# A list scheduler counts 32-wide matmuls at a quarter of their work, sends outputs ahead at low activity, and gets new settings per stretch

## The chip, the cores and the metric

The kernel runs on one core of one Trainium2 chip. The metric is the time of one execution on the device, in microseconds (us). The kernel before takes 723.09 us, the median of 3 runs (721.96 to 723.36).

## What is computed

The reference is an attention stage with 32 inducing vectors, done twice, and then a gated feed-forward layer on its output:

```python
B, N, m, C = (4, 12416, 32, 128)
def mab(q, kv):
    s = scale * (q @ kv.transpose(0, 2, 1))
    s = s - s.max(-1, keepdims=True)
    a = np.exp(s)
    a /= a.sum(-1, keepdims=True) + 1e-09
    return a @ kv
h = mab(I, x)             # I: 32 inducing vectors for each of 4 batches
attn = mab(x, h)          # 4 * 12416 rows of 128
gate = 1.0 / (1.0 + np.exp(-(attn @ w_gate)))    # w_gate, w_val: 128 x 1536
val = attn @ w_val
return (gate * val @ w_out).astype(np.float32)   # w_out: 1536 x 128
```

Since `attn` is `a2 @ h`, the kernel multiplies the 32-row `h` by the weights once for each batch (`hw`, made at L395) and multiplies the 32 attention weights `a2` of each row by that.

## The kernel before

**The tiles.** The 49664 rows are 96 blocks of 512 rows, and a 97th of what is left over (128 rows of each batch). A block has 12 chunks (`NJ`), each 128 of the 1536 hidden columns. A chunk goes through four engines:

- PE (TensorE) makes `v_ps` and `g_ps`, one matmul each with 32 rows of contraction, 128 columns of weights and 512 moving columns (a "fill", `emit_fill`, L1178);
- ACT (ScalarE) takes the tanh of `g_ps` into `t` (L1192);
- DVE (VectorE) makes `u = (t + 1) * v` (`emit_product`, L1204), straight from PSUM;
- PE adds the chunk into the block's output with four 128x128x128 matmuls (`acc_ps`, `emit_out`, L1229). When all 12 chunks are in, ACT copies the block out at half its value (L1246) and SP stores it (L1253).

Chunks are taken in steps of two and one by turns (`step`, L1339): a step of two has one product of 128x1024, a step of one a product of 128x512. Each size has one PSUM buffer for `v` and one for `g`, so a fill of a size waits until the product before it of that size has been read. If two chunks are left at the end, the last step departs from the turns.

**Side work.** Between the blocks of one batch the first stage of the next batch is done: scores of 16 tiles of rows (`s_ps`, L294, 32 columns of weights and 512 moving columns), maximum, exp, a transpose by DMA, and sums (`hp_ps`, L354, 128 rows of contraction, 32 columns of weights; with each of 128 moving columns goes one of a single column). Then the second-stage weights `a2` of the batch's groups of four blocks are made on PE, ACT and POOL (GpSimd), and SP transposes them by DMA into `a2r` (L571), which the fills read. Some chunks are put "aside" (`maybe_aside`, L1513): their product is made by ACT and POOL instead of DVE (`side_g_ps`, `side_v_ps` at L1555, `side_t` at L1565 to L1576). There are 23 of these.

**What sets the order.** All of this is issued by a list scheduler that runs when the kernel is built. It keeps a model clock for each engine and calls `do_pe`, `do_act`, `do_dve` and so on for the engine that is free first; the instructions are then emitted in order of their modelled start. Each engine's queue runs in that order on the chip. The rules are steered by numbers (`knob`), which `SETTINGS` changes at every eighth block (`STRETCH = 8`). In `do_pe` (L1760) the order of choice is: fills that are due, then side work (`side_`), then output matmuls (`run_out`), then a "pulse" (`emit_pulse`, L1742: a matmul of zeros into the open output bank). `queued() > knob["outq"]` makes outputs `pressed`: they then go ahead of side work, unless that has waited longer than `age`.

A pulse is sent when PE has nothing to do and `recent(tau)` (L1752) is below `guard`. `recent` sums the `work` of the PE operations that started in the last 3413 ns:

```python
for start, work in reversed(spent):
    if start < tau - 3413:
        break
    busy += work
```

The `work` of an output matmul is 0.95 of its cost of 56, which is 53; a fill is counted at 53 for each chunk; a group's scores at 852, half a group's sums at 430 (8 matmuls of 128 moving columns and 8 of one), half of `hw` at 850.

Of the kernel before, what the change touches and what calls it, by code (L numbers as in the profile page):

```python
# [21 lines left out]
SWAPS = True  # L22
STRETCH = 8
SETTINGS = (
    dict(most=6, margin=300, loose=150, lead=1000, calm=26, outq=40, quiet=1, slack=90,
        guard=1800, hold=22, eager=300, keep=0, pace=9999, soft=80, push=36, patience=6000,
        hurry=100, window=320, age=3500, ahead=21),
    dict(quiet=3, push=14),
    dict(eager=100, push=30),
    dict(lead=1900, quiet=1, eager=300, soft=20, push=36),  # L30
    dict(soft=80),
    dict(),
    dict(),
    dict(calm=22),
    dict(calm=26, hold=26),
    dict(hold=22, push=26),
    dict(push=36),
    dict(),
)
TIMES = (  # L40
# [36 lines left out]
def kernel(  # L77
# [508 lines left out]
    early, middle, last = arrival[:EARLY], arrival[EARLY:-1], arrival[-1]  # L586
# [246 lines left out]
    ROW, COL, FULL = "row", "col", "full"  # L833
    SWITCH = 100
    FILL = 216
# [13 lines left out]
    knob = dict(SETTINGS[0])  # L849
# [46 lines left out]
    def add(eng, cost, lag, emit, deps=(), after=None, kind=FULL, opens=False, closes=False, rank=None, work=None):  # L896
        op = Op(eng, cost, lag, emit, deps, after, kind, work=work)
        op.opens, op.closes = opens, closes
        op.rank = len(ranks) if rank is None else rank
        ranks.append(op)  # L900
        wait[eng].append(op)
        for d in op.deps:
            if d.done is None:
                d.users.append(op)
                op.left += 1
        if op.left == 0:
            live[eng].append(op)
        return op
# [27 lines left out]
    loaded, turned, hw_op, hT_op, a2_op, s1_used = {}, {}, {}, {}, {}, {}  # L936
# [3 lines left out]
    def op_stage1(b, s, score_at, sum_at, st):  # L940
        full = groups[s][1] == GC
        ng, w, R = s1_dims(s)

        def score():
            st["s1"] = s1_score_pe(b, s, "m")

        def weigh():
            st["a1T"] = s1_exp(b, s, st["s1"])

        a = add("PE", FILL, 380, score, [turned[b, s]], score_at, COL, opens=True, work=852)  # L950
        heads.append(a)
        n = 512 if full else 128
        m_ = add("DVE", 64 + 1.047 * n, 84 + 1.047 * n, lambda: s1_max(b, s, st["s1"]), [a])
        x = add("ACT", 600 if full else 250, 700 if full else 342, weigh, [m_], closes=True)
        if full:
            def turn():
                st["a1"] = s1_turn_dma(b, s, st["a1T"])
            c = add("SP", 80, 3400, turn, [x])
        else:
            def turn_pe():  # L960
                st["aT"] = s1_turn_pe(b, s, st["a1T"])
            def turn_copy():
                st["a1"] = s1_turn_copy(s, st["aT"])
            t_ = add("PE", 60, 240, turn_pe, [x], None, FULL, opens=True)
            heads.append(t_)
            c = add("DVE", 81, 160, turn_copy, [t_], closes=True)

        def part(k0, k1):
            if k0 == 0:
                st["hp"] = side_tile([P, C + 1], F32, "hp_ps")  # L970
            s1_sum_pe(b, s, st["a1"], st["hp"], k0, k1)

        p0 = add("PE", 160, 300, lambda: part(0, 2), [c, loaded[b, s]], sum_at, COL, opens=True, work=430)
        heads.append(p0)
        p1 = add("PE", 160, 300, lambda: part(2, 4), [p0], None, COL, work=430) if full else p0
        s1_used[b, s] = add(
            "ACT", 147, 260, lambda: s1_sum_keep(b, s, st["hp"]), [p1], closes=True
        )

    def op_combine(b, join_at, total_at, fill_at):  # L980
# [44 lines left out]
        def part(hf):  # L1025
            st["hw_ps"] = hw_fill(b, hf, side["m"])
# [8 lines left out]
        a = add("DVE", 71, 160, least, [s1_used[b, s] for s in range(NS)], join_at)  # L1035
# [10 lines left out]
        )  # L1046
        last = None
        for hf in range(2):
            f = add("PE", 170, 330, lambda hf=hf: part(hf), [hT_op[b], last], fill_at[hf], COL, opens=True, work=850)
            heads.append(f)  # L1050
            last = add("ACT", 360, 485, lambda hf=hf: keep(hf), [f], closes=True)
        hw_op[b] = last
# [699 lines left out]
    def recent(tau):  # L1752
        busy = 0
# [4 lines that stand above are left out]
        return busy  # L1758

    def do_pe(tau):  # L1760
# [7 lines left out]
        if rG is not None and (nxt["G"] < 2 or (st is None)):  # L1768
            s = max(tau + pe_switch(ROW), rG)
# [11 lines left out]
        if rG is not None and sg["n"] < nxt["V"] + 2 and rG <= tau + pe_switch(ROW):  # L1781
            s = max(tau + pe_switch(ROW), rG)
# [4 lines left out]
        for o in live["PE"]:  # L1787
            r = ready(o)
# [103 lines left out]
```

## Time and profile before

| | before |
|---|---|
| median of 3 runs | 723.09 us |
| the profiled execution, its own time | 717.5 us |
| its span, first to last instruction | 715.7 us |
| mean granted TensorE clock | 0.994 |
| DVE busy, share of the span | 98% |
| ACT busy | 95% |
| PE busy | 98% |
| POOL busy | 67% |
| SP's stores of a block, issue to landing | 2.2 us |

The profiled execution is 5.6 us shorter than the median of the runs. In a row of a group, the number after the bar is the group's busy time in us, then the mean of one instruction in ns, then the time that the engine stood idle before these instructions, with what ended it. In a table of stretches, each engine has its busy time in us in the stretch and in brackets the instructions that reach into it; PEclk is the granted clock of the stretch.

### The profile page before, as it was taken

Reading aid. Unit: us, or ns where it says so; the run is one execution under the profiler, and the core shown is the slowest. Engines: PE = TensorE matmul, PEld = TensorE weight load, DVE = VectorE, ACT = ScalarE, POOL = GpSimd, SP = SyncE. Lnnn points to the kernel's source line nnn. Section 1 sums busy time; section 2 is a strip of 40 time slices with the busy share of each in tenths; the row PEclk is TensorE's granted clock in tenths of the full one; section 3 lists DMA queues with packets and bytes.
Section 4 is the critical chain, followed back from the end, with each engine's and each line's share of the span. In section 5 each row is a group of like instructions: output and inputs, shape, how many; then the busy total and the mean of one; then the engine's idle time right before and its main releaser. Section 6 shows DMA issues by size and latency. Waiting matters only on the chain.

```text
span 715.7 us, 21551 instructions
## 1 busy us (share of the span) xinstructions
PE 700.7 (98%) x8449; PEld 408.2 (57%) x8449; DVE 698.1 (98%) x862; ACT 677.8 (95%) x1037; POOL 483.0 (67%) x747
## 2 busy tenths in 40 slices
PE   8999999999999999999999999999999999999997
PEld 4455565555555555555555655565555555555555
DVE  6899999999999999999999998999999999999997
ACT  4699999999999999999999998999999999999996
POOL 4587586688776774879895582777677588588211
PEclk9999999999999999999999998999999999999999
DMA  9797596225377625242357623121221120320211
GB/s 210 114 187 140 115 164 133 61 75 102 94 156 140 116 69 112 68 104 69 89 99 161 123 47 60 60 62 45 67 71 60 46 76 30 76 69 37 77 45 46
DMA packets 118181, 65.76 MB, mean 92 GB/s; under 512 B 101408, under 2 KB 102208, under 8 KB 118080
## 3 DMA queue, kind: packets, MB, share of 16 engines
q1 hardware_dynamic: 112176, 50.90, 30.5%
q0 software_dynamic: 5584, 13.34, 11.7%
q8 instruction: 66, 1.08, 0.6%
q14 instruction: 35, 0.29, 0.1%
q10 hardware_dynamic: 320, 0.15, 0.1%
HBM read 27.80 MB, written 25.43 MB: 74 GB/s over the span
## 4 chain that ended last, share of the span: by engine, by line
PE 83%; DVE 6%; ACT 5%; DMA 3%; issue 2%; POOL 1%; DVEq 0%; ACTq 0%; POOLq 0%
PE acc_ps L1229 41%; PE v_ps L1178 31%; PE g_ps L1178 6%; DVE u L1204 5%; ACT t L1192 5%; PE s_ps L429 2%; DMA xn<-in_x_dram 2%; PE hp_ps L354 1%; DMA a2r<-a2n 1%; PE s_ps L294 1%; PE side_g_ps L1555 0%; DVE nm L306 0%; PE xt_ps L615 0%; ACT o L1246 0%; POOL hpart L658 0%
## 5 line engine op out<-in xcount | busy, mean ns | idle before, releaser
L1204 DVE SCALAR_TENSOR_TENSOR u<-t,v_ps 128x1024 f16<-128x1024 f16 x761 | 666.3, 948 | 3.4 <-PE g_ps L1178 2.0
L1192 ACT ACTIVATE t<-g_ps 128x1024 f16<-128x1024 f32 x760 | 583.4, 832 | 16.9 <-ACT t L1192 5.8
L1229 PE MATMUL acc_ps<-wo,u 128*128 128x128 f16 x4564 | 389.3, 221 | 0.9 <-ACT o L1246 0.5
L1229 PEld LDWEIGHTS <-u 128*128 128x128 f16 x4564 | 262.6, 98 | 165.7 <-issue 162.8
L1178 PE MATMUL v_ps<-a2r,hwt 32*128 32x512 f16 (+1 forms) x1165 | 292.2, 377 | 5.2 <-DVE u L1204 2.0
L1178 PE MATMUL g_ps<-a2r,hwt 32*128 32x512 f16 (+1 forms) x1165 | 290.8, 375 | 0.0
L1178 PEld LDWEIGHTS <-hwt 32*128 32x128 f16 x2354 | 103.5, 91 | 98.7 <-issue 15.9
L560 POOL TENSOR_TENSOR a2n<-e,rs 128x2048 f16<-128x2048 f16 (+1 forms) x23 | 83.9, 3648 | 1.8
L533 POOL TENSOR_TENSOR near<-sme,minus 128x16 f32<-128x16 f32 (+1 forms) x22 | 65.2, 2964 | 1.8
L1246 ACT ACTIVATE o<-acc_ps 128x512 f32<-128x512 f32 x96 | 58.5, 610 | 0.0
L484 POOL TENSOR_SCALAR rise<-rise 128x256 f32<-128x256 f32 (+6 forms) x110 | 51.0, 463 | 9.4
L482 POOL TENSOR_TENSOR rise<-sc 128x256 f32<-128x256 f32 (+1 forms) x22 | 16.2, 737 | 58.2 <-ACT sc L472 58.1
L1576 POOL TENSOR_TENSOR side_t<-side_t,side_v 128x512 f16<-128x512 f32 x23 | 29.2, 1267 | 33.3 <-ACT side_v L1573 17.7
L1569 POOL TENSOR_SCALAR side_t<-side_t 128x512 f32<-128x512 f16 x23 | 34.4, 1497 | 19.4 <-ACT side_t L1565 19.2
L508 POOL TENSOR_TENSOR sum<-e 128x256 f32<-128x256 f16 (+1 forms) x23 | 15.4, 671 | 35.6 <-ACT e L500 33.4
L486 POOL TENSOR_TENSOR top<-top,rise 128x128 f32<-128x128 f32 (+3 forms) x88 | 28.3, 322 | 7.1
L508 POOL TENSOR_TENSOR sum<-sum 128x128 f32<-128x128 f32 (+3 forms) x92 | 28.3, 308 | 7.0
L482 POOL TENSOR_TENSOR rise<-top 128x128 f32<-128x128 f32 (+3 forms) x88 | 27.2, 309 | 6.7
L490 POOL TENSOR_TENSOR sc<-sc,top 128x512 f32<-128x512 f32 (+1 forms) x22 | 23.8, 1084 | 1.7
L319 ACT ACTIVATE a1T<-s_ps,nm 128x512 f16<-128x512 f32 (+1 forms) x26 | 16.9, 651 | 3.0 <-DVE nm L306 2.9
L429 PE MATMUL s_ps<-hT,xT 128*128 128x32 f16 x388 | 17.8, 177 | 0.1
L429 PEld LDWEIGHTS <-xT 128*128 128x128 f16 x388 | 14.0, 96 | 6.5 <-issue 6.1
(157 smaller groups left out, 340.9 us busy)
## 6 DMA issues: line engine op xcount, KB each, us to landing
out_dram<-o SPq DMA_DIRECT2D x96, 256.0 KB, 2.2
xn<-in_x_dram POOLq DMA_DIRECT2D x18, 512.0 KB, 6.9
xn<-in_x_dram POOLq DMA_DIRECT2D x3, 544.0 KB, 7.6
xn<-in_x_dram POOLq DMA_DIRECT2D x3, 256.0 KB, 12.6
xn<-in_x_dram SPq DMA_DIRECT2D x1, 576.0 KB, 4.9
xn<-in_x_dram SPq DMA_DIRECT2D x1, 512.0 KB, 4.0
a2r<-a2n SPq DMA_TRANSPOSE x27, 4.5
wg<-in_moe_w_gate_dram POOLq DMA_DIRECT2D x1, 384.0 KB, 11.6
```

What stands on the lines that cost most here:

```text
L429: nc.tensor.matmul(s2[:, j, :], xT[b][:, c + j, :], hT16[b][:], start=(j == 0), stop=whole and j == j1 - 1, skip_group_check=True,)
L482: nc.gpsimd.tensor_tensor(out=r, in0=far, in1=near, op=ALU.subtract)
L484: nc.gpsimd.tensor_scalar_max(out=r, in0=r, scalar1=0.0)
L508: nc.gpsimd.tensor_tensor(out=d[:, 0:n, :], in0=src[:, :, 0:w], in1=src[:, :, w : 2 * w], op=ALU.add)
L533: nc.gpsimd.tensor_tensor(out=near[:, 0:n], in0=sme[:, 0:n], in1=minus1[:, 0:n], op=ALU.pow)
L560: eng.tensor_tensor(out=a2n[:, 0:n, :, :], in0=e.unsqueeze(2).to_broadcast((P, n, 4, m)), in1=rs.unsqueeze(2).unsqueeze(3).to_broadcast((P ...
L1178: nc.tensor.matmul(pt[:, k, col : col + nb * P], hw[b][r : r + 32, j // 2, :], a2r[r : r + 32, o : o + nb, :].rearrange("p j t -> p (j t)" ...
L1192: st["tanh"] = nc.scalar.activation(out=st["t"][:], in_=st["g"][:], func=AF.Tanh, scale=0.5)
L1204: u = nc.vector.scalar_tensor_tensor(out=st["u"][:, :, c:e], in0=st["t"][:, :, c:e], scalar=1.0, in1=st["v"][:, :, c:e], op0=ALU.add, op1= ...
L1229: nc.tensor.matmul(accs[i][(q // 2) % len(accs[i])][:, q, :], u[:, ts(q, P)], wo16[:, item["j"], :], start=begins, stop=last, skip_group_c ...
L1246: nc.scalar.mul(out=o32[:], in_=accs.pop(i)[0][:], mul=0.5)
L1569: nc.gpsimd.tensor_scalar_add(out=st["t1"][:], in0=st["t"][:], scalar1=1.0)
```

## The change

The change does four things, all in the scheduler:

- a group's scores count 213 instead of 852, half a group's sums 107 instead of 430, half of `hw` 160 instead of 850: rows times columns of the array, as fills were counted already;
- outputs are also `pressed` when `recent(tau)` is below a new knob `warm` (1500, and 1700 in one stretch);
- the numbers in `SETTINGS` are chosen anew: among others `guard` is 1700 in the first stretch and then 1800, `lead` 1900 for nearly all of the way (which puts chunks aside only when ACT is that far ahead), and `age` 2500 in the first;
- with these, 24 chunks are put aside instead of 23, at other places, and the order of nearly every stretch differs.

```diff
 SETTINGS = (
-    dict(most=6, margin=300, loose=150, lead=1000, calm=26, outq=40, quiet=1, slack=90,
-        guard=1800, hold=22, eager=300, keep=0, pace=9999, soft=80, push=36, patience=6000,
-        hurry=100, window=320, age=3500, ahead=21),
...
+    dict(most=6, warm=1500, margin=300, loose=150, lead=1900, calm=26, outq=40, quiet=1,
+        slack=90, guard=1700, hold=22, eager=300, keep=0, pace=9999, soft=80, push=26,
+        patience=6000, hurry=100, window=320, age=2500, ahead=21),
...
-        a = add("PE", FILL, 380, score, [turned[b, s]], score_at, COL, opens=True, work=852)
+        a = add("PE", FILL, 380, score, [turned[b, s]], score_at, COL, opens=True, work=213)
...
-        p0 = add("PE", 160, 300, lambda: part(0, 2), [c, loaded[b, s]], sum_at, COL, opens=True, work=430)
+        p0 = add("PE", 160, 300, lambda: part(0, 2), [c, loaded[b, s]], sum_at, COL, opens=True, work=107)
...
-        p1 = add("PE", 160, 300, lambda: part(2, 4), [p0], None, COL, work=430) if full else p0
+        p1 = add("PE", 160, 300, lambda: part(2, 4), [p0], None, COL, work=107) if full else p0
...
-            f = add("PE", 170, 330, lambda hf=hf: part(hf), [hT_op[b], last], fill_at[hf], COL, opens=True, work=850)
+            f = add("PE", 170, 330, lambda hf=hf: part(hf), [hT_op[b], last], fill_at[hf], COL, opens=True, work=160)
...
-        pressed = r is not None and r <= tau + 30 and queued() > knob["outq"]
+        pressed = r is not None and r <= tau + 30 and (queued() > knob["outq"] or recent(tau) < knob["warm"])
```

In the whole program PE has 4656 output matmuls as before (96 of them from chunks aside, before 92), two fills less at L1178 and two more at L1555, and 13 pulses instead of 3. Seven of the pulses, of 512 columns each, stand between the fills near the end of block 83 (counted from 0), just ahead of the four output matmuls of a chunk aside. DVE has 380 products of 128x1024 and 379 of 128x512 as before, and the last step has one chunk instead of two.

**PE, in the first stage of the last batch (block 56 counted from 0; now 56 and 57), two groups' sums.** `hp_ps_9660` and `hp_ps_9714` are the sums of two groups, `u16_...` a product, `hwt` and `a2r` what the fills read. Before:

```order
L1229 MATMUL acc_ps_9590<-wo16_108,u16_9607 128x128
...
L354 MATMUL hp_ps_9660<-xn_3_5414,a1_9404 32x128
...
L1178 MATMUL v_ps_9679<-a2r_9118,hwt_7620 128x512
...
L354 MATMUL hp_ps_9660<-ones16_121,a1_9404 32x1
...
L1178 MATMUL v_ps_9702<-a2r_9118,hwt_7620 128x512
...
L354 MATMUL hp_ps_9714<-xn_3_5414,a1_9519 32x128
...
L1229 MATMUL acc_ps_9590<-wo16_108,u16_9621 128x128
L1178 LDWEIGHTS hwt_7620
L1178 MATMUL v_ps_9734<-a2r_9118,hwt_7620 128x512
```

The same two groups now (here `hp_ps_9718` and `hp_ps_9814`):

```order
L354 MATMUL hp_ps_9718<-ones16_121,a1_9310 32x1
L1229 LDWEIGHTS u16_9663
L1229 MATMUL acc_ps_9604<-wo16_108,u16_9663 128x128
L1178 LDWEIGHTS hwt_7480
L1178 MATMUL v_ps_9776<-a2r_9265,hwt_7480 128x512
...
L1229 MATMUL acc_ps_9604<-wo16_108,u16_9675 128x128
...
L1229 MATMUL acc_ps_9787<-wo16_108,u16_9702 128x128
...
L1229 MATMUL acc_ps_9787<-wo16_108,u16_9715 128x128
...
L354 MATMUL hp_ps_9814<-xn_3_5378,a1_9539 32x128
```

Before, the second group's sums follow the first's with one step's fills between them and no output matmul, and one output matmul stands in the middle of the second group. Now 16 output matmuls stand between the two groups, and one between the halves of each.

**DVE, the end of the program.** The rows are the last products and the last copy out. Before:

```order
L1204 SCALAR_TENSOR_TENSOR u16_15562<-t16_15524,v_ps_15555 128x512
L1204 SCALAR_TENSOR_TENSOR u16_15590<-t16_15550,v_ps_15564 128x1024
L1204 SCALAR_TENSOR_TENSOR u16_15623<-t16_15587,v_ps_15611 128x2x384
L1204 SCALAR_TENSOR_TENSOR u16_15623<-t16_15587,v_ps_15611 128x2x128
L1243 TENSOR_SCALAR o32_15651<-acc_ps_15584 128x256
```

Now:

```order
L1204 SCALAR_TENSOR_TENSOR u16_15611<-t16_15555,v_ps_15584 128x512
L1204 SCALAR_TENSOR_TENSOR u16_15625<-t16_15582,v_ps_15613 128x1024
L1204 SCALAR_TENSOR_TENSOR u16_15646<-t16_15608,v_ps_15629 128x384
L1204 SCALAR_TENSOR_TENSOR u16_15646<-t16_15608,v_ps_15629 128x128
L1243 TENSOR_SCALAR o32_15669<-acc_ps_15596 128x256
```

Before, two steps of two chunks follow each other; now the last step has one chunk and follows a step of two.

**SP, at the transposes for the last batch (around the 48th store).** SP's queue holds the stores of blocks (`out_0_dram<-o32`), the transposes `xT` of the last batch's input and the transposes `a2r` for the fills. Before:

```order
L1253 DMA out_0_dram<-o32_8192 128x512
L145 DMA_TRANSPOSE xT_3_8267<-xn_3_5414 128x16x128 x2
L1253 DMA out_0_dram<-o32_8376 128x512
L571 DMA_TRANSPOSE a2r_8418<-a2n_8348 128x16x128
L145 DMA_TRANSPOSE xT_3_8267<-xn_3_5414 128x16x128
L1253 DMA out_0_dram<-o32_8505 128x512
```

Now:

```order
L1253 DMA out_0_dram<-o32_8353 128x512
L145 DMA_TRANSPOSE xT_3_8256<-xn_3_5378 128x16x128 x2
L1253 DMA out_0_dram<-o32_8479 128x512
L571 DMA_TRANSPOSE a2r_8523<-a2n_8445 128x16x128
L145 DMA_TRANSPOSE xT_3_8256<-xn_3_5378 128x16x128
L1253 DMA out_0_dram<-o32_8617 128x512
```

The rows read alike, but `o32_8376` is the 48th store and `o32_8479` the 49th: this `a2r` comes one store later. Its first reader on PE stands after 51.10 blocks' worth of output matmuls before and after 50.92 now. Of the 22 other `a2r` of four blocks, 18 stand behind the same store as before, two behind one later and two behind one earlier.

More of the change, by code (lines that the diff above doesn't have):

```diff
@@ L24 @@
 SETTINGS = (
-    dict(most=6, margin=300, loose=150, lead=1000, calm=26, outq=40, quiet=1, slack=90,
-        guard=1800, hold=22, eager=300, keep=0, pace=9999, soft=80, push=36, patience=6000,
-        hurry=100, window=320, age=3500, ahead=21),
[L28 to L31, printed above, removed]
+    dict(most=6, warm=1500, margin=300, loose=150, lead=1900, calm=26, outq=40, quiet=1,
+        slack=90, guard=1700, hold=22, eager=300, keep=0, pace=9999, soft=80, push=26,
+        patience=6000, hurry=100, window=320, age=2500, ahead=21),
+    dict(guard=1800, push=36, age=3500),
     dict(),
     dict(),
[L34 to L37, printed above, removed]
+    dict(warm=1700, slack=60),
+    dict(warm=1500, margin=260, slack=90, eager=200),
+    dict(lead=1000, quiet=0, slack=60),
+    dict(margin=300, lead=1900, quiet=1, eager=100, push=14),
+    dict(outq=56, quiet=0, slack=90, soft=60, push=36),
+    dict(calm=30),
+    dict(hold=18, push=20, window=200),
     dict(),
```

## The prediction

> **What bounds the kernel now.** I read the page's first part, then the groups of DVE by shape, then a table of long stretches.
>
> ```profile
> PE 700.7 (98%) x8449; PEld 408.2 (57%) x8449; DVE 698.1 (98%) x862; ACT 677.8 (95%) x1037; POOL 483.0 (67%) x747
> L1204 DVE SCALAR_TENSOR_TENSOR u<-t,v_ps 128x1024 f16<-128x1024 f16 x380 | 462.2, 1216 | 2.4 <-PE g_ps L1178 1.8
> L1204 DVE SCALAR_TENSOR_TENSOR u<-t,v_ps 128x512 f16<-128x512 f16 x379 | 257.9, 680 | 0.4 <-PE g_ps L1178 0.2
> L1204 DVE SCALAR_TENSOR_TENSOR u<-t,v_ps 128x768 f16<-128x768 f16 x1 | 1.0, 955 | 0.6 <-PE v_ps L1178 0.6
> L1204 DVE SCALAR_TENSOR_TENSOR u<-t,v_ps 128x256 f16<-128x256 f16 x1 | 0.4, 416 | 0.0
> 40.00:250.00 210.00, 206.72 (x2564) 120.85 (x2562) 209.78 (x248) 205.09 (x314) 154.97 (x240) 1.00 0.64 122
> 250.00:251.00 1.00, 1.00 (x16) 0.59 (x13) 0.48 (x2) 1.00 (x3) 0.67 (x1) 1.00 0.47 169
> 251.00:433.80 182.80, 181.70 (x2243) 105.86 (x2241) 182.79 (x217) 179.40 (x275) 136.06 (x208) 1.00 0.45 95
> 433.80:444.00 10.20, 10.20 (x102) 5.46 (x101) 8.34 (x12) 7.94 (x13) 0.14 (x1) 0.67 0.19 52
> 444.00:709.00 265.00, 263.07 (x3072) 154.14 (x3072) 264.74 (x307) 259.58 (x388) 170.85 (x253) 1.00 0.20 57
> 709.00:715.70 6.70, 2.71 (x43) 2.01 (x40) 2.03 (x4) 0.64 (x2) 0.00 (x0) 0.85 0.23 74
> ```
>
> The third busy number of a stretch is DVE. From 40 us to 709 us it works without a pause except at two places: 0.52 us lost at 250 us, and 10.20 - 8.34 = 1.86 us lost from 433.8 to 444 us. Elsewhere it loses 0.22 + 0.01 + 0.26 = 0.49 us in 658 us. DVE's products are the bound, so the change can pay only where DVE stands, where it gets less to do, or at the two ends. The start (the prologue) is not touched. Since PE and ACT stand behind DVE, their 98% and 95% are no separate bound.
>
> **Why DVE stands at 433.8 us.** The granted clock falls to 0.5 for 6.8 us there. I cut the time into pieces of 3.4 us, first all engines, then PE's output matmuls (L1229), fills (L1178), sums (L354) and scores (L294) alone:
>
> ```profile
> 266.60:270.00 3.40, 2.77 (x34) 1.69 (x31) 3.40 (x7) 3.24 (x7) 1.23 (x1) 1.00 0.64 126
> 430.40:433.80 3.40, 3.38 (x68) 1.57 (x65) 3.40 (x5) 3.40 (x7) 3.32 (x3) 1.00 1.20 155
> 433.80:437.20 3.40, 3.40 (x38) 1.44 (x37) 3.02 (x5) 3.21 (x6) 0.14 (x1) 0.50 0.37 81
> 437.20:440.60 3.40, 3.40 (x28) 1.97 (x24) 2.18 (x3) 1.70 (x3) 0.00 (x0) 0.50 0.00 0
> 440.60:444.00 3.40, 3.40 (x44) 2.06 (x40) 3.14 (x5) 3.03 (x5) 0.00 (x0) 0.99 0.20 73
> ```
>
> ```profile
> 427.00:430.40 3.40, 2.02 (x27) 1.34 (x24) 1.00 0.01 2
> 430.40:433.80 3.40, 0.77 (x5) 0.36 (x5) 1.00 1.20 155
> 259.70:263.10 3.40, 0.84 (x9) 0.40 (x7) 1.00 0.20 77
> ```
>
> ```profile
> 430.40:433.80 3.40, 2.10 (x14) 0.60 (x12) 1.00 1.20 155
> 259.70:263.10 3.40, 2.26 (x12) 0.65 (x12) 1.00 0.20 77
> ```
>
> ```profile
> 430.40:433.80 3.40, 0.97 (x48) 0.60 (x48) 1.00 1.20 155
> 259.70:263.10 3.40, 0.65 (x32) 0.40 (x32) 1.00 0.20 77
> ```
>
> ```profile
> 259.70:263.10 3.40, 0.18 (x4) 0.10 (x4) 1.00 0.20 77
> ```
>
> PE is busy 3.38 of 3.40 us just before the fall, but with 5 output matmuls where the piece before had 27. Weighed with the numbers of the scheduler's code, this piece has 5 x 53 + 14 x 53 + 3 halves of a group's sums (16 matmuls each). With the old 430 for a half that is 2297, above `guard` 1800, so the old rules saw nothing to mend; with the new 107 it is 1328, below `warm` 1500. The poorest other piece that I found, at 259.7 us, has 9 x 53 + 12 x 53 + 2 x 107 + 213 = 1540 by the new count and kept its clock. So the edge at which the clock falls lies between 1328 and 1540 of the new count, and `warm` and `guard` lie at its upper end. The piece at 266.6 us kept its clock with PE idle for 0.63 us of it, so idle time alone does not do it.
>
> [...]
>
> **Part by part.** Four terms, on the profiled execution of 717.5 us (span 715.7).
>
> *The count and the pressed outputs.* In the order after, 16 output matmuls stand between the two groups' sums where there were none, and one between the halves of each group. 16 x 53 = 848 lies between the sums, so a piece as poor as 1328 is not formed there, and the clock stays: DVE's 1.86 us come back. The bounds: nothing, if the fall stays or moves, and 1.86 us, all that DVE lost. I take 1.86. What is pressed aside for it is the sums and scores, which wait at most `age` behind outputs; POOL, their next user, works 67% of the span, which covers that. If the cover is gone, an `a2r` comes late (a rival).
>
> *The last step.* 24 chunks aside leave 1140 for DVE, so the last step has one chunk. Before, its 768 and 256 wide products took 0.955 + 0.416 us. For 384 and 128 I go down the line from 1216 (1024 wide) to 680 (512), 1.047 ns a column: 0.546 + 0.278 us. That is 0.55 us less. Ahead of it DVE stood still:
>
> ```profile
> DVE u L1204 <- PE v_ps L1178: 0.6, 1, 0.6
> 709.92 1.29 DVE L1204 SCALAR_TENSOR_TENSOR u<-t,v_ps 128x768 f16<-128x768 f16 x2 [0.60 <-PE v_ps L1178]
> 711.64 0.39 ACT L1241 ACTIVATE o<-acc_ps 128x256 f32<-128x256 f32 x1 [2.38 <-PE acc_ps L1229]
> ```
>
> Two steps of two chunks in a row share one PSUM buffer, so the last `v_ps` could be filled only after the product before had ended. The last step of one chunk uses the other buffer, whose reader ended a product earlier; the 0.60 us go. Next late is PE with its output matmuls, which now has 32 of them behind the last fill (27 before, when they ended 0.4 us behind DVE): it may keep 0.1 or 0.2 us of this, which I leave to the range. Together 1.15 us, between 0.55 and 1.15.
>
> *The wait at 250 us.* The fill of a chunk aside waited for its `a2r`, whose DMA took 9.0 us:
>
> ```profile
> 240.18 9.01 DMA a2r<-a2n
> 249.24 0.37 PE L1555 MATMUL side_g_ps<-a2r,hwt 32*128 32x512 f16 x1 [0.20 <-DMA a2r<-a2n]
> 250.58 1.82 DVE L1204 SCALAR_TENSOR_TENSOR u<-t,v_ps 128x1024 f16<-128x1024 f16 x2 [0.52 <-PE g_ps L1178]
> DMA to landing us min/median/max: 2.9/4.4/9.6
> ```
>
> That chunk stands elsewhere now, so these 0.52 us go. But the 24 new places are a new draw of the same kind, and one such accident in 23 is what the trace shows: I take 0, between -0.52 and +0.52.
>
> *Pulses and the 24th chunk.* Pulses are sent only where the plan has PE idle until the next fill.
>
> ```profile
> L1743 PE MATMUL acc_ps<-wo,zero 128*128 128x512 f16 x1 | 0.4, 390 | 0.0
> L1565 ACT ACTIVATE side_t<-side_g_ps 128x512 f16<-128x512 f32 x23 | 13.7, 598 | 0.1
> L1573 ACT COPY side_v<-side_v_ps 128x512 f32<-128x512 f32 x23 | 13.6, 593 | 0.0
> L1192 ACT ACTIVATE t<-g_ps 128x512 f16<-128x512 f32 x379 | 235.7, 622 | 0.3 <-PE g_ps L1178 0.3
> ```
>
> The seven pulses in block 83 fill the time in which PE's outputs wait for POOL's `side_t`; at 0.39 us each they cost 2.7 us if nothing covered them, and nothing if PE stands there anyway. I take nothing, which is nearer since the fills between them keep their turns. The 24th chunk adds 0.60 + 0.59 us to ACT and takes one tanh share of some 0.62 us away: 0.6 us more of 38 us that ACT is idle. Nothing.
>
> The sum: 1.86 + 1.15 = 3.01 us, about 3.0 less: 714.5 for an execution like the profiled one. The median of the runs stands 5.6 us above the profiled execution, and no row here says why; I take that part as the same after: 723.09 - 3.0 = 720.1 us.
>
> **The rivals.** Anything within 0.2% (1.45 us) is about what a measurement of this kernel can't tell from no change.
>
> *The clock paid nothing in the median run.* The poor stretch is barely longer than the 3.4 us piece that I cut at the fall. [...] Against: the profiled run, which is faster than all three, had the fall. Then only the last step pays: 723.09 - 1.15 = 721.9. [...] Chance 0.20.
>
> *The fall has another cause.* Thin work is not the cause, say; the fall stays, and with it its 1.86 us: also 721.9. Against it is the row of 5 output matmuls. [...] Chance 0.05.
>
> *More falls in the runs than in the profile.* The 5.6 us would be three falls of 1.86. If two further ones were there and go, 3.0 + 3.7 = 6.7 less, 716.4. Only the sum speaks for it. Chance 0.10.
>
> *New waits eat the gain.* Nearly every stretch is ordered anew, and DVE loses 0.49 us outside the named places now; if accidents like that at 250 us came six times, 723.2. Against: 23 chunks aside gave one. Chance 0.10.
>
> *Slower: an `a2r` comes late for its block.* SP's rows of the last batch's transposes, and the first reader on PE:
>
> ```profile
> 376.13 1.96 SPq L571 DMA_TRANSPOSE a2r<-a2n  x1
> 378.18 3.24 SPq L145 DMA_TRANSPOSE xT<-xn  x1
> 382.18 0.34 SPq L1253 DMA_DIRECT2D out_dram<-o  x1
> 394.44 0.39 PE L1178 MATMUL g_ps<-a2r,hwt 32*128 32x512 f16 x2
> DMA to landing us min/median/max: 2.3/4.6/13.8
> ```
>
> The last row is that of the `xT` transposes, which share the queue. This `a2r` moves behind the next store, from 376.1 to 382.5 us, and its first reader 0.18 block of some 7 us earlier, to 393.2. It costs from the point where it lands more than 10.7 us after its issue. The longest `a2r` took 9.6 us, the longest `xT` 13.8: that would hold PE, and all fills behind, for 3.1 us. With a clock term that pays nothing, 721.9 + 3.1 = 725.0. Chance 0.10.
>
> **How the numbers follow.** My forecast has 0.45; its own range is 719.6 (the wait at 250 us gone for good, 0.52) to 721.2 (one more such wait, and 0.55 instead of 1.15 from the last step). The range of 8 in 10 leaves out the two outer rivals with their 0.20. It goes down to 717.2, which is one further fall avoided (1.86), the 0.52 and the other 0.49 us of waits, and up to 723.3, the new waits. Faster: 0.43 of my forecast, a third of the two rivals at 721.9 (0.25), since that is just inside the bound, 0.10 from more falls, and 0.02 of the new waits: 0.63. Slower: 0.10 from the late `a2r` and 0.04 of the rest. Same: 0.23.
>
> **What would show it.** Right: a PEclk row without a 0.5 after the start, DVE busy the whole of the stretch where the last batch's sums stand, no wait for `v_ps` at the end, last products of about 546 and 278 ns, a span near 712.7 us. The count is wrong if the clock falls at a place that weighs over 1540, or if a fall remains at the sums. The late `a2r` would show as PE waiting for the DMA near 393 us, new waits as rows of DVE waiting for `g_ps` elsewhere.

## The result and the profile after

The changed kernel takes 713.96 us, the median of 4 executions (713.85 to 716.65), against 722.53 (721.47 to 723.36) for the kernel before beside it: a ratio of 0.989, with a 95% interval of 0.986 to 0.992. That is 8.6 us less, where 3.0 were forecast. A repeat of 12 executions gave 714.22 us (713.59 to 715.05) and 0.991 (0.988 to 0.994). The ratios leave out executions that lie over 1.5% above a kernel's own best, so where a kernel has such ones the counts are given too.

The profiled execution is the slowest of the four. The page's first part and the groups of DVE's products by shape:

```profile
PE 699.5 (98%) x8459; PEld 405.7 (57%) x8459; DVE 697.8 (98%) x862; ACT 677.8 (95%) x1039; POOL 485.5 (68%) x749
L1204 DVE SCALAR_TENSOR_TENSOR u<-t,v_ps 128x1024 f16<-128x1024 f16 x380 | 462.2, 1216 | 1.5 <-PE g_ps L1178 0.8
L1204 DVE SCALAR_TENSOR_TENSOR u<-t,v_ps 128x512 f16<-128x512 f16 x379 | 257.8, 680 | 1.3 <-PE hp_ps L354 1.3
L1204 DVE SCALAR_TENSOR_TENSOR u<-t,v_ps 128x384 f16<-128x384 f16 x1 | 0.5, 549 | 0.0
L1204 DVE SCALAR_TENSOR_TENSOR u<-t,v_ps 128x128 f16<-128x128 f16 x1 | 0.3, 281 | 0.0
```

DVE's work is what it was, but for the last step: 549 and 281 ns, where 546 and 278 were forecast, and no idle time ahead of them. The table of long stretches of this execution, and what PE waited for at its one accident:

```profile
40.00:248.40 208.40, 204.88 (x2529) 118.83 (x2527) 207.08 (x245) 202.92 (x310) 154.21 (x238) 1.00 0.62 123
248.40:252.40 4.00, 4.00 (x35) 2.07 (x32) 3.10 (x4) 3.06 (x6) 2.20 (x6) 0.57 0.17 68
433.80:444.00 10.20, 10.20 (x161) 5.66 (x158) 10.20 (x13) 10.16 (x18) 6.33 (x6) 1.00 0.41 104
444.00:709.00 265.00, 262.57 (x3089) 153.17 (x3088) 264.78 (x308) 259.99 (x390) 173.39 (x255) 1.00 0.20 58
```

```profile
PE hp_ps L354 <- DMA a<-a1T: 1.3, 1, 1.3
```

From 433.8 to 444 us DVE, the third busy number, now works 10.20 of 10.20 us and the clock stays at 1.00: the fall that the prediction spoke of is gone. Ahead of 248 us a transpose came late for a group's sums; DVE lost 1.3 us up to 248.4 us and 0.9 behind it, with a clock of 0.57. So this execution has a new fall, and it misses the prediction's sign of a clock row without a 0.5. In the profiled execution of the repeat (its span is 712.5 us) this accident is missing too:

```profile
248.40:252.40 4.00, 3.98 (x52) 2.52 (x50) 4.00 (x6) 3.85 (x7) 2.37 (x6) 1.00 0.17 66
433.80:444.00 10.20, 10.20 (x176) 5.98 (x172) 10.17 (x14) 10.20 (x19) 4.44 (x3) 1.00 0.36 80
```

At their places the named terms look as forecast: 714.5 us, the prediction's figure for an execution like the profiled one, lies near the 713.96 that were measured. What is gone besides is the 5.6 us by which the profiled execution of before (717.5 us) lay under its median, and which the prediction took to be the same after.

### The profile page after: what moved, and what is told of

It reads as the page before. It is cut to its first block, busy times and chain, and to the rows that moved or that the text cites. A ratio compares the mean times of both kernels' runs of the same rounds, so it can differ in the third digit from the quotient of the medians.

```text
span 714.8 us, 21586 instructions
## 1 busy us (share of the span) xinstructions
PE 699.5 (98%) x8459; PEld 405.7 (57%) x8459; DVE 697.8 (98%) x862; ACT 677.8 (95%) x1039; POOL 485.5 (68%) x749
## 4 chain that ended last, share of the span: by engine, by line
PE 83%; DVE 6%; ACT 6%; DMA 2%; issue 1%; POOL 1%; DVEq 0%; ACTq 0%; POOLq 0%
PE acc_ps L1229 40%; PE v_ps L1178 31%; PE g_ps L1178 6%; ACT t L1192 5%; DVE u L1204 5%; PE s_ps L429 2%; DMA xn<-in_x_dram 2%; PE hp_ps L354 1%; DMA a<-a1T 1%; PE s_ps L294 1%; PE acc_ps L1743 0%; PE side_g_ps L1555 0%; ACT o L1246 0%; PE xt_ps L615 0%; POOL hpart L658 0%
## 5 line engine op out<-in xcount | busy, mean ns | idle before, releaser
L1229 PE MATMUL acc_ps<-wo,u 128*128 128x128 f16 x4560 | 387.0, 221 | 0.8 <-ACT o L1246 0.5
L1229 PEld LDWEIGHTS <-u 128*128 128x128 f16 x4560 | 262.2, 98 | 163.8 <-issue 161.3
L1178 PE MATMUL v_ps<-a2r,hwt 32*128 32x512 f16 (+1 forms) x1164 | 291.3, 376 | 4.4 <-DVE u L1204 2.1
L1178 PE MATMUL g_ps<-a2r,hwt 32*128 32x512 f16 (+1 forms) x1164 | 289.9, 374 | 0.0
L1178 PEld LDWEIGHTS <-hwt 32*128 32x128 f16 x2352 | 100.6, 91 | 99.2 <-issue 18.6
L1569 POOL TENSOR_SCALAR side_t<-side_t 128x512 f32<-128x512 f16 x24 | 35.9, 1495 | 19.1 <-ACT side_t L1565 11.4
```

Source lines behind the costliest of these rows:

```text
L1178: nc.tensor.matmul(pt[:, k, col : col + nb * P], hw[b][r : r + 32, j // 2, :], a2r[r : r + 32, o : o + nb, :].rearrange("p j t -> p (j t)" ...
L1229: nc.tensor.matmul(accs[i][(q // 2) % len(accs[i])][:, q, :], u[:, ts(q, P)], wo16[:, item["j"], :], start=begins, stop=last, skip_group_c ...
L1569: nc.gpsimd.tensor_scalar_add(out=st["t1"][:], in0=st["t"][:], scalar1=1.0)
```

## The experiments

The medians hide a spread. Of 149 further executions of the kernel before, 30 took under 716.5 us, 12 took 716.5 to 719, and 107 took 719 or more.

My first theory was that of the prediction, thin work on PE and the falls of the clock that follow. Its rival: the new order took away waits that the clock has no part in.

**The kernels again, and one part alone.** Both kernels as they are (before_again, after_again):

> The kernel before itself, to see the granted clock of every run. Theory A (falls of the clock): the runs at some 722.5 us have about three falls more than the profiled one of 717.5 us; a fall of 6.8 us at half clock takes 0.0048 off the mean clock, so they show 0.994 - 3 x 0.0048 = about 0.980, and time and clock go together over the runs (1.9 us for 0.0048). Theory B (the new order removes waits that have nothing to do with the clock): the runs show 0.994 as the profiled one, and their times don't follow the clock. Both: 721.5 to 723.5 us, ratio 1.00.

> The changed kernel itself. Theory A: clock 0.999 to 1.000 in runs at 714 us, and a run near 716.7 us is one with a fall (0.996). Theory B: times spread without the clock. Both: ratio 0.987 to 0.991.

Before took 721.31 us (715.11 to 725.01), and two of 12 executions were under 716.5; after took 714.22, all 12 of them under 715.1. The profiled execution of before_again took 720.21 us. It has the fall of the first profile, a little later, and DVE lost 1.86 us in it:

```profile
436.00:444.00 8.00, 8.00 (x86) 4.12 (x84) 6.14 (x8) 5.74 (x10) 0.66 (x1) 0.57 0.42 42
```

The rest of what it took above 715 us is several short waits. The old settings with the new counts (before_warm), and with pulses wherever PE has nothing to do (before_pulses):

```diff
-        a = add(... score_at, COL, opens=True, work=852)
+        a = add(... score_at, COL, opens=True, work=213)
...
-        pressed = r is not None and r <= tau + 30 and queued() > knob["outq"]
+        pressed = r is not None and r <= tau + 30 and (queued() > knob["outq"] or recent(tau) < 1500)
```

> The kernel before with the new counts and with outputs ahead of side work below 1500, but the old settings: 23 chunks aside and the old last step, so 1.15 us of the gain are missing. Theory A: most falls go, and the runs take 722.5 - 7.4 = 715 to 717 us at a clock of 0.99 or more. Theory B: the settings carry the gain, so it stays at 721 to 723 us.

```diff
-        if i < NB - 1 and todo[i] < NJ and tau > 4000 and recent(tau) < knob["guard"]:
+        if i < NB - 1 and todo[i] < NJ and tau > 4000 and recent(tau) < 9999:
```

> The kernel before with its old counts and settings, but a pulse of zeros wherever PE has nothing to do in the plan (18 instead of 3). Theory A: pulses stand only where PE idles, which is not where sums and scores fill it, so at most one fall goes: 720 to 722.5 us. Theory B: 722 to 723 us, the same as before.

before_warm: 722.55 us (717.10 to 724.03), ratio 1.001 (0.997 to 1.005). before_pulses: 726.72 us (722.00 to 731.31), ratio 1.008 (1.004 to 1.011). Its order differs from the first pulse on, so it isn't a test of the pulses alone. The theory of thin work fell here as the main cause, by before_warm. But before_warm emits the same order as before up to some 430 us on every engine, so its trace shows what an execution of the kernel before can do there. Its table of stretches, its longest wait of PE, and two answers on its transfers, those issued from 90 to 105 us and the `xT` issued at 86 us (the last number of such a row is the median from issue to landing in us):

```profile
84.00:107.00 23.00, 20.98 (x278) 12.63 (x277) 21.87 (x28) 21.77 (x35) 19.05 (x32) 1.00 1.14 97
107.00:114.80 7.80, 4.38 (x34) 2.63 (x34) 2.72 (x4) 1.85 (x3) 2.63 (x8) 0.56 1.00 162
```

```profile
PE s_ps L294 <- DMA xT<-xn: 5.2, 1, 5.2
```

```profile
out_dram<-o SPq DMA_DIRECT2D x2, 256.0 KB, 19.1
a<-a1T SPq DMA_TRANSPOSE x1, 21.0
```

```profile
xT<-xn SPq DMA_TRANSPOSE x1, 24.4
```

PE stood 5.2 us for that `xT`, DVE lost 1.13 + 5.08 = 6.2 us up to 114.8 us, and the clock fell behind the standstill, to a mean of 0.56. In after_again the same stretches, and the same transfers:

```profile
84.00:107.00 23.00, 22.48 (x279) 12.93 (x278) 23.00 (x30) 22.57 (x37) 18.53 (x28) 1.00 1.05 177
107.00:114.80 7.80, 7.80 (x111) 4.27 (x110) 7.72 (x10) 7.35 (x12) 6.02 (x15) 1.00 0.30 77
```

```profile
out_dram<-o SPq DMA_DIRECT2D x2, 256.0 KB, 4.3
...
a<-a1T SPq DMA_TRANSPOSE x1, 5.4
```

```profile
xT<-xn SPq DMA_TRANSPOSE x1, 11.1
```

The last two columns of a stretch are the DMA share and GB/s: the DMA share is above 1 in both (1.14 and 1.05), but 97 GB/s are moved in the one and 177 in the other. Stores land after 19 us instead of 4. I call this the jam: `xT` and a1 transposes and stores from SP meet three loads of `xn` that POOL issues (in before at 86.5, 89.9 and 99.9 us). In the quoted profile of before, the `xT` issued at 86 us landed after 13.8 us, some 5 us ahead of its reader.

A late transfer isn't the only way in which PE stands there. In before_again and in before_pulses, in this order, PE stopped at 105 us in the middle of a chunk's output matmuls; "issue" means that the profile shows nothing that it waited for:

```profile
PE acc_ps L1229 <- issue: 1.5, 1, 1.5
PE acc_ps L1229 <- issue: 5.2, 1, 5.2
```

What held PE there stays open. No execution of before itself near its median of 722.5 us was profiled; how the jam costs such an execution its time is read from before_warm and from kernels below that differ from before on SP's queue alone.

**The order on SP's queue.** The changed kernel has the store ahead of the a1 transpose near 84 us and the next `xT` ahead of a store near 94 us; before has them the other way round. The next four kernels move only SP's queue, or only two of POOL's loads; PE, ACT and DVE keep their order.

```diff
+    moved = [k for k in planned if order[k].eng == "SP"]
+    order[moved[16]].start = order[moved[15]].start - 1
+    planned = sorted(range(len(order)), key=lambda k: (order[k].start, k))
```

> The kernel before with two neighbours on SP's queue exchanged, as the change has them: the store of a block ahead of the transpose of a1, so that the store is not right ahead of the xT transpose issued near 86 us. All other queues as before. Theory J (that xT transpose is jammed by the transfers around it, lands after its reader's turn on PE near 105 us, and PE, DVE and the clock follow): if the store right ahead of it is what jams, most runs take 714.5 to 718 us, median under 718. Theory L (the load of xn that starts with it jams it, whatever the store does): 721 to 723 us, as before. Theory A (thin stretches of work alone): 721 to 723 us.

The same with 21 ahead of 20, which is the pair near 94 us:

> The kernel before with two other neighbours on SP exchanged, as the change has them: the next xT transpose (near 98 us) ahead of a store. Theories J and L: the first transpose is jammed before this one is issued, so little changes, 720 to 723 us; if the queue's later part makes the jam, under 718. Theory A: 721 to 723 us.

Before with two of the `xn` loads, from 89.9 and 99.9 us, 17 to 20 us later (at 109.4 and 116.7):

```diff
-LOADS = ((33, 37, 60, 60, 78, 82), (24, 33, 42, 60, 60, 82))
+LOADS = ((44, 48, 60, 60, 78, 82), (24, 33, 42, 60, 60, 82))
```

> The kernel before with two loads of xn for the batch after next moved on POOL's queue from near 90 and 100 us to some 3 blocks later. PE, DVE, ACT and SP as before. Theory L: the jam near 86 to 110 us goes, the xT lands in 5 to 14 us, and the runs take 714.5 to 718 us. Theory J with the store: still jammed, 720 to 723 us. Theory A: 721 to 723 us.

And the changed kernel with both pairs put back:

```diff
+    moved = [k for k in planned if order[k].eng == "SP"]
+    order[moved[15]].start = order[moved[16]].start + 1
+    order[moved[20]].start = order[moved[21]].start + 1
+    planned = sorted(range(len(order)), key=lambda k: (order[k].start, k))
```

> The changed kernel with both pairs on SP put back in the order that they have before; nothing else. Theory J: the slow runs come back, median 718 to 722 us. Theories L and A: 714 us, as the changed kernel.

store_first took 715.13 us: 9 of 12 executions at 714.6 to 716.1, three at 723 to 729; ratio 0.992 (0.988 to 0.996). xt_first alone did nothing: 723.25 us, 1.000 (0.995 to 1.004). The profiled executions of store_first (723.23 us, one of its three) and of xt_first (722.16) have the jam; here it is an `a2r` that comes late, and PE's longest waits are, in this order:

```profile
PE g_ps L1178 <- DMA a2r<-a2n: 5.7, 1, 5.7
PE g_ps L1178 <- DMA a2r<-a2n: 4.7, 1, 4.7
```

late_loads took 714.95 us, nine of ten under 715.7 and one at 717.33; ratio 0.991 (0.988 to 0.994). Its trace still has the `xT` of 86 us landing after 16.0 us and 109 GB/s from 90 to 105 us; what is gone is PE's wait, since the `a2r` behind them, issued at 104.4 us, lands after 4.9. after_reversed lost it all: 723.94 us, three of 12 under 716 and nine at 722 to 730. In its trace, the longest wait of PE and the stretches from 110 us:

```profile
PE g_ps L1178 <- DMA a2r<-a2n: 7.1, 1, 7.1
```

```profile
110.00:115.00 5.00, 3.52 (x55) 2.09 (x51) 4.81 (x6) 3.20 (x6) 2.79 (x8) 1.00 1.06 48
115.00:120.00 5.00, 0.00 (x0) 0.00 (x0) 0.00 (x0) 0.00 (x0) 0.00 (x0) 0.52 1.15 152
120.00:140.00 20.00, 19.39 (x168) 10.21 (x168) 12.35 (x14) 13.29 (x20) 9.34 (x11) 0.52 0.19 56
```

All engines stand from 115 to 120 us, while an `a2r` issued at 105.2 us is on its way, and the clock is at half for most of 20 us. Two swaps on SP's queue, nothing else, bring this back: that the order on SP's queue brings the wait and takes it away is shown. Are the two pairs all of it? both_first puts both into the kernel before:

> The kernel before with both pairs of SP's queue turned round, the store ahead of the a1 transpose near 84 us and the next xT ahead of a store near 94 us. If these two pairs are all that the change does to the crowd of transfers, no execution is left at 721 or above: about 715 us, 714.4 to 717.5, ratio 0.990. If the first pair alone only made the crowd rarer by chance of timing, it stays like that kernel: most at 715, some 3 in 12 at 721 to 729.

715.28 us, ratio 0.995 (0.990 to 0.999), with nine of 12 under 716 and one at 717.28, but two at 724 and 732, which were not profiled. By these times the jam is rarer by the two pairs and not gone, and two of 12 against store_first's three doesn't tell whether the second pair adds anything. The changed kernel had none in 16 executions. What else of its order keeps it out stays open.

**The settings alone, and the loads once more.** The changed kernel with the old counts and without `warm` (settings_alone), and as it is with the later loads (after_late):

```diff
-        pressed = ... (queued() > knob["outq"] or recent(tau) < knob["warm"])
+        pressed = ... (queued() > knob["outq"])
```

> The changed kernel with the old counts of work and without the new rule for pressed outputs; its first 32 blocks are ordered as in the changed kernel on SP, so the stores and transposes near 85 us stand as there. If the crowd of transfers near 85 to 105 us is what cost the kernel before its 7 us or so, this kernel keeps the whole gain: about 714 us, nearly all executions between 713.6 and 717, ratio about 0.989. If the new counts and pressed outputs are what saves the clock, it loses the gain: 720 us or more.

> The changed kernel with two loads of xn issued some three blocks later, which alone took the kernel before to 714.95 us. If both edits remove the same crowd of transfers, they don't add up: about 713.9 us, 713.5 to 714.5, the same as the changed kernel. If the loads cost something by themselves (a second cause), it is faster than the changed kernel by some of the 7 us, below 711.

Both missed: 728.5 us (727.56 to 730.12), ratio 1.012 (1.007 to 1.018), and 722.44 us (720.31 to 723.05), 1.004 (1.001 to 1.008). The table of settings_alone, from the place of the jam to its bad one:

```profile
84.00:120.00 36.00, 35.63 (x454) 20.19 (x453) 35.92 (x45) 35.08 (x57) 25.84 (x44) 1.00 0.74 138
120.00:643.60 523.60, 519.16 (x6249) 301.99 (x6247) 523.14 (x616) 511.11 (x775) 386.81 (x603) 1.00 0.37 84
643.60:647.00 3.40, 2.97 (x21) 1.16 (x19) 3.40 (x5) 3.09 (x5) 3.24 (x3) 1.00 0.00 0
647.00:650.40 3.40, 3.28 (x21) 1.40 (x21) 2.78 (x5) 2.72 (x5) 0.91 (x1) 0.50 0.40 77
650.40:664.00 13.60, 13.60 (x66) 4.99 (x66) 7.26 (x8) 7.22 (x10) 1.26 (x1) 0.50 0.17 42
```

The jam is away, as expected, and DVE loses 0.54 us from 84 to 643.6 us. Its SP queue has the changed kernel's order up to 296 us, while before_warm, with the new counts, has the old one there: the order that keeps the jam away comes with the new settings, not with the counts. Then comes a piece of 3.4 us with 21 matmuls, and the clock falls and stays at half for 17 us. DVE loses 7 us from 643.6 to 664 us, and the mean clock of this execution, 0.981, is below the 0.987 or so that this fall alone would leave (an estimate: half of 17 us in 728.3, from 0.999), so that more is lost elsewhere. after_late is alike: moving the loads made the scheduler order later blocks anew. Its pieces ahead of the fall and in it, and of the first piece the output matmuls (L1229) and the fills (L1178) alone:

```profile
611.60:615.00 3.40, 2.91 (x21) 1.16 (x20) 3.40 (x5) 3.09 (x5) 0.00 (x0) 1.00 0.80 154
615.00:618.40 3.40, 3.35 (x22) 1.48 (x22) 2.50 (x3) 2.64 (x5) 0.00 (x0) 0.50 0.20 77
```

```profile
611.60:615.00 3.40, 0.99 (x9) 0.47 (x7) 1.00 0.80 154
```

```profile
611.60:615.00 3.40, 2.35 (x12) 0.69 (x13) 1.00 0.80 154
```

With 9 outputs and 12 fills it weighs 21 x 53 = 1113, less than the 1328 at which the clock fell in before.

So thin work does cost, under the new settings: they need the new counts and pressed outputs, though these alone gain nothing on the old settings. To move nothing but the loads, after_loads shifts them in the finished order:

```diff
+    for g in (0, 1):
+        loaded[2, g].start += 22000
```

> The changed kernel with the same two xn loads issued some 22 us later on POOL's queue, and no other instruction moved. If the stores' and transposes' new places had already removed the crowd of transfers, nothing is left to gain: 713.5 to 714.3 us, the clock at 1. If the loads still cost something, it is faster than 713.5.

716.63 us (715.46 to 719.37): neither. The `xT` at 86 us landed after 8.8 us instead of 11.1, but the loads, now at 112.4 and 123.8 us, met a later a1 transpose. The longest wait of PE, and the stretch:

```profile
PE hp_ps L354 <- DMA a<-a1T: 1.6, 1, 1.6
```

```profile
129.00:135.00 6.00, 4.42 (x88) 2.73 (x86) 4.54 (x7) 4.58 (x9) 1.37 (x7) 1.00 0.68 139
```

DVE lost 1.46 us there. A load moved out of one crowd made another. The new counts with the jam away, on late_loads (late_counts):

> The kernel before with the two xn loads later (714.95 us by itself) and the new counts with outputs pressed below 1500. The clock's fall at 434 us, which was in about one execution in ten of that kernel at 717 us, should go by the prediction's first term; the median stays at 714.9 us (714.4 to 715.3), since most executions did not have the fall. If the new counts bring more, the median goes below 714.4.

715.01 us (714.62 to 715.66), ratio 0.995 (0.991 to 0.998), none at 717. One execution of ten in late_loads and none of 12 here is no proof that the counts remove the fall, but the medians agree: where the jam is away, the clock term of the prediction is worth nothing in the median. Of the six traces in which PE has the old order of 434 us, before and before_again have the fall, and store_first, xt_first, both_first and late_loads keep their clock there, by an estimate from their mean clocks. Such a fall takes some 0.0048 off (6.8 us at half clock in 715.7). both_first has 0.998 and late_loads 0.999; store_first and xt_first have 0.995, of which the fall at 115 to 125 us takes 0.0047 (a clock of 0.77 and 0.55, and of 0.64 and 0.68, in pieces of 5 us).

**The last step.** after_23 makes no 24th aside:

```diff
-        if i >= NB - 1 or len(asides[i]) >= knob["most"]:
+        if i >= NB - 1 or len(asides[i]) >= knob["most"] or sum(map(len, asides.values())) >= 23:
```

> The changed kernel with 23 chunks aside: the last of the 24 goes back to DVE, so the last two steps have two chunks each as before the change. The term of the last step (0.55 us for one chunk fewer and 0.60 us for the wait for v_ps) says 715.1 us, 1.15 us more than the changed kernel's 714.0. If the last 16 and more output matmuls set the end anyway, about 0.1 to 0.5 us more, 714.3.

715.01 us (714.83 to 715.68), 1.05 more than the changed kernel's 713.96 and 0.8 more than the 714.22 of its repeat. The wide product and the wait are back, in the group of DVE and in its list of waits:

```profile
L1204 DVE SCALAR_TENSOR_TENSOR u<-t,v_ps 128x768 f16<-128x768 f16 x1 | 1.0, 953 | 0.6 <-PE v_ps L1178 0.6
```

```profile
DVE u L1204 <- PE v_ps L1178: 0.6, 1, 0.6
```

**What the clock counts.** All four of these are the changed kernel, with the pulses changed and nothing moved. Without the last nine (no_block83), on 32 columns of the array (thin_pulses), on 32 rows (row_pulses), and cut to 128 moving columns (short_pulses):

```diff
+        if hasattr(order[k], "pulse") and order[k].start > 500000:
+            continue
```

> The changed kernel without its last nine pulses, the seven in block 83 (621.6 to 625.6 us) among them; nothing else moves. PE then has about 13 fills and no output matmul in some 3.4 us. If thin work makes the clock fall, it falls there for 6.8 us and DVE stands for 2 to 5 us: 716 to 719 us. [...]

```diff
-            accs[i][0][:, 0 : n // P, :],
-            zero16[:],
+            accs[i][0][0:32, 0 : n // P, :],
+            zero16[:, 0:32],
```

> The changed kernel with every pulse on 32 columns of the array instead of 128: the same count, the same 512 moving columns, PE as busy as before, a quarter of rows times columns. If rows times columns is what counts, the clock falls near 622 us as without the pulses: 716 to 719 us. If it is enough that PE is busy, the clock stays: 714.0 us.

```diff
-            zero16[:],
-            wo16[:, 0 : n // P, :],
+            zero16[0:32],
+            wo16[0:32, 0 : n // P, :],
```

> The changed kernel with every pulse on 32 rows of the array instead of 128, all 128 columns, as many moving columns as before. If rows times time is what the clock counts, the piece at 621.6 us weighs 13 x 53 + 7 x 53 = 1060, as poor as any that fell, and the clock falls as without the pulses: 715.2 to 720 us. If the time in which the array streams is what counts, the clock stays: 714.0 us.

```diff
     def emit_pulse(i, n):
+        n = min(n, 128)
```

> The changed kernel with every pulse cut to 128 moving columns, on the whole array: a quarter of the streaming time. By rows times time, and by streaming time, it is poor (7 x 53 ns in place of 7 x 213): the clock falls near 622 us, 715.2 to 720 us, as without the pulses. If a matmul now and then is enough, the clock stays: 714.0 us.

no_block83: 715.92 us (715.19 to 719.74). thin_pulses: 714.01 (713.76 to 714.41). row_pulses: 715.84 (715.22 to 717.37, 6 executions). short_pulses: 716.85 (714.84 to 720.26). The pieces 621.6 to 625 and 625 to 628.4 us of after_again, no_block83, thin_pulses and row_pulses:

```profile
621.60:625.00 3.40, 3.40 (x19) 0.88 (x16) 3.38 (x5) 3.40 (x6) 3.40 (x2) 1.00 0.00 0
625.00:628.40 3.40, 3.40 (x38) 1.89 (x37) 3.40 (x4) 3.36 (x6) 3.15 (x6) 1.00 0.00 0
```

```profile
621.60:625.00 3.40, 2.93 (x13) 0.73 (x13) 3.40 (x5) 3.40 (x6) 3.40 (x3) 0.87 0.00 0
625.00:628.40 3.40, 3.40 (x25) 1.56 (x22) 2.66 (x4) 3.03 (x5) 3.15 (x5) 0.50 0.00 0
```

```profile
621.60:625.00 3.40, 3.40 (x21) 0.98 (x18) 3.38 (x5) 3.40 (x7) 3.40 (x2) 1.00 0.00 0
625.00:628.40 3.40, 3.40 (x38) 1.88 (x35) 3.40 (x5) 3.36 (x7) 3.15 (x6) 1.00 0.00 0
```

```profile
621.60:625.00 3.40, 3.35 (x19) 0.98 (x18) 3.30 (x4) 3.40 (x6) 3.40 (x3) 0.68 0.00 0
625.00:628.40 3.40, 3.40 (x24) 1.43 (x18) 2.52 (x4) 2.66 (x5) 3.15 (x5) 0.50 0.00 0
```

Pulses on a quarter of the columns held the clock at 1.00, as whole ones did; on a quarter of the rows they didn't (0.68 and 0.50), though PE was busy 3.35 of 3.40 us. My expectation for thin_pulses, by rows times columns, fell. In the first piece the pulses (L1743) are busy for 2.15 us in row_pulses and for 1.94 us in after_again.

## Why the prediction was wrong

*DVE is the bound, and gains come only where it stands.* Right: its work is the same to 0.3 us, and the differences that the traces above show are stretches in which it stood, or its last products.

*"The median of the runs stands 5.6 us above the profiled execution, and no row here says why; I take that part as the same after."* This step failed. Those 5.6 us come from the jam near 85 to 120 us, whose cost the one profiled execution had escaped: the 30 executions of before under 716.5 us have a median of 715.07, the profiled one lies 2.4 above them with its fall at 434 us, and the median execution some 7.5. How the 7.5 divide into PE's wait, the fall of the clock behind it and smaller waits differs from trace to trace. Two orders on SP's queue bring the jam and take it away. With the loads later, too, PE doesn't wait, at 714.95 us, 7.6 below 722.5, and with the last step's 0.8 to 1.05 that is 8.4 to 8.65, where 8.6 were measured and 8.3 in the repeat. What a single profile lacks can't be held constant. That the changed kernel has the order without the jam is luck: nothing in the change aims at it, and the rows of SP's queue above show only the last batch, where the pairs of 84 and 94 us don't stand.

*The late `a2r`.* The mechanism was right, and placed wrongly on both counts. I looked for it near 393 us as a loss of the new order; it stood in the old order near 107 to 120 us, as a gain to be had. The row that I quoted for it, `xT` landing after 2.3 to 13.8 us with 4.6 in the middle, was its trace: the 13.8 is that `xT` at 86 us, and the 24.4 of before_warm makes PE stand. POOL's loads, on a queue of their own, bear on it: that `xT` landed after 11.1 us in after_again and after 8.8 in after_loads, where two of them come later, and with the loads elsewhere PE's wait ends (late_loads, 714.95 us against 722.5), or moves (after_loads, 1.6 us for an a1 transpose).

*More falls in the runs than in the profile*, 716.4 us at 0.10. Nearest in size, and wrong in kind: the traces of 722 to 728 us (xt_first, store_first, after_reversed) have one fall before the end, as the profile has, but behind a standstill of PE for a transfer (4.7, 5.7 and 7.1 us), not at thin work. In before_again, at 720.21 us, there is only the known fall.

*The count and the pressed outputs*, 1.86 us. Right at its place in the profile (DVE 10.17 to 10.20 of 10.20 us), and late_loads' one execution at 717.33, at a mean clock of 0.994, lies 2.4 us above its median. But late_counts against late_loads is worth nothing in the median, and four of six traces with the old order have no such fall. So the rival that the clock pays nothing in the median run was right where the jam is away, and there the term should have been about 0; for the median of before itself this isn't shown. No run shows by what means an execution keeps its clock at 434 us: what they show is that the same order kept its clock there in four traces and lost it in two (a mean of 0.67 from 433.8 to 444 us in before, of 0.57 from 436 to 444 us in before_again).

*The fall's cause.* Two falls came behind standstills of PE: of 5.2 us in before_warm (a clock of 0.56 from 107 to 114.8 us) and of 7.1 us in after_reversed (0.52 from 115 to 140 us). Those at 434 us in before and at 622 us in row_pulses did not: PE was busy 3.38 of 3.40 us just ahead of the one and 3.35 of 3.40 us in the piece in which the other begins. Thin work is the cause at 622 us, as the pulses show (715.92 us without them, 714.22 with them), and the nearest reading at 434 us, where PE was as busy; but four traces with the same thin work there keep their clock.

*The last step*, 1.15 us: 0.8 to 1.05 measured, with products of 549 and 281 ns. What is lacking is near the 0.1 to 0.2 that I left to PE's outputs; DVE now waits 0.7 us for them ahead of the last copy, 0.5 before.

*The wait at 250 us*, taken as 0 within 0.52: in the profiled execution a wait for another transpose came ahead of 248 us and cost 1.3 + 0.9 us with the fall behind it, in the repeat none. A size off, and it goes with the 716.65 of one in four.

*Pulses cost nothing.* Right, but their cost was the wrong question: without the last nine the kernel loses 1.96 us in the median. They fill a place in block 83 that is poor only in the new order; before had no pulse there and no fall.

## What to carry to other kernels

Where the profiled execution lies well below the median of the runs, ask what it escaped before holding that gap constant: look for the transfer whose time to landing has a long tail, and whose reader would stand for it. Here transposes and stores on one queue and loads on another jammed together, and the order of two neighbours in a queue was worth more (715.13 us in store_first, against 722.5) than the new counts alone (722.55); moving loads away helped where they met no other crowd (714.95 us in late_loads) and not where they did (716.63 in after_loads). So the order on the queues deserves a look beside the compute plan. A plan's settings and its cost counts belong together: here each half alone gained nothing or lost 6 us, and both together gained 8.6.

## What the runs showed of the hardware

- Near 622 us in the changed kernel, the granted clock of the two pieces of 3.4 us from 621.6 us was 1.00 and 1.00 with the seven pulses whole (714.22 us in the median), and the same with them on 32 of 128 columns (714.01). It was 0.68 and 0.50 with them on 32 rows (715.84), 1.00 and 0.61 with short ones (716.85), and 0.87 and 0.50 without them (715.92).
- That rows of the array times time decide there is the author's estimate from these five kernels, no more. Four sums on 32 columns each start within some 10 ns of each other (before, 431.72 us: 0.24 us for the four, 0.23 for one). By that estimate they count as one, and the changed code's number for them would be right, though not for the reason of rows times columns; this wasn't tested by itself.
- By the numbers of the changed code, pieces of 3.4 us lost the clock at 1113 (611.6 us in after_late, PE busy 2.91 us) and at 1328 (430.4 us in before, PE busy 3.38). But the same order at 434 us kept its clock in four of six traces, so such a piece didn't always lose it; why was not tried, nor where an edge lies up to the 1540 that kept it (259.7 us in before).
- A DMA share above 1 did not tell that much was moved: 97 GB/s at 1.14 (before_warm, 84 to 107 us) and 177 GB/s at 1.05 (after_again). Why the first mix moves so little was not tried.
